# A five-stage network on one core: two weight matrices are converted to float pairs in pieces of 512 columns in place of 256

## The chip, the cores and the metric

The kernel runs on one core of a Trainium2 chip. The metric is the device time of one execution in microseconds (us); the time before is 730.76 us, the median of three runs (730.09 to 730.91). The engines are TensorE (PE in the profile: matrix products; PEld: its weight loads), VectorE (DVE), ScalarE (ACT), GpSimd (POOL) and SyncE (SP), which here does nothing but issue transfers between HBM and the on-chip memory.

## The reference

Three blocks follow one another on 8 sequences of 576 tokens with 512 features. Attention has no softmax: per head `kv = k^T v`, `o = q kv`, and `o` is scaled by the reciprocal root of its mean square. A gated block multiplies `x @ w_val` by the sigmoid of a causal convolution of 5 taps and applies `w_out`. A spatial gating block applies `w_in`, gelu, normalises one half, mixes it over the tokens by `w_sg`, multiplies the other half by it, applies `w_out2` and adds its input:

```
kv = einsum('bhsd,bhse->bhde', k, v);  out = einsum('bhsd,bhde->bhse', q, kv)
x  = out / sqrt(mean(out*out) + 1e-6) * g_norm
x  = (sigmoid(conv5(x)) * (x @ w_val)) @ w_out
h  = gelu(x @ w_in);  u, v = h[:512], h[512:]
v  = w_sg @ normalised(v) + b_sg
return x + (u * v) @ w_out2
```

`w_in` is 512 x 1024 and `w_out2` 512 x 512. They, like `w_val` and `w_out`, come as 64-bit floats.

## The kernel before

TensorE multiplies numbers of a reduced width, so each operand is held as a pair (high and low part), and a product takes three passes (`gemm3`, L228). A 64-bit weight is loaded as pairs of 32-bit words into a tile `raw` (two buffers) and turned into such a pair by `split` in eight steps on a work tile `cv` (one buffer): on ScalarE L131, on VectorE L141, L142 and L134, on ScalarE L178 (the high part is written), on VectorE L143 and L138, on GpSimd L186, and on VectorE L188 (the low part is written). One piece is 128 rows by `WC` columns. `split` returns the load of a piece first and its steps second, so `wi[n][0]()` issues a load and `wi[n][1]()` the steps.

The first part of the kernel is a loop over 8 sequences (b = 0 to 7), each in 8 slots (s = 0 to 7). In slots 0 to 3 PE computes a block of 128 features of `x @ w_val` (val), in slots 4 to 7 one of the product with `w_out` (y). Between these stands the attention of the next sequences: products with k and v (kv, L280), `o` for one tile of 128 tokens (L296), its square on ScalarE (L302), the sum over heads on VectorE (L305), mean and power on GpSimd (L306, then L307), the scaling back on VectorE (L310, which writes a tile T), and the transposes on PE (xT, L325). ScalarE and VectorE take the transposed tile over (L329, L330, L334). When the fifth tile of a sequence is there, ScalarE makes the first tap of its convolution (L353) and VectorE the other four: 16 instructions of line L359 that follow one another, the burst spoken of below. VectorE further does L387 (val times gate) and L391 (low parts; half of these on GpSimd). After b = 3 and b = 7 comes a tail, in which the last 64 tokens of four sequences are handled together (256 columns wide).

Pieces of `w_in` and `w_out2` are converted in the slots that a table gives for each b; their loads are issued two pieces ahead, into the two buffers of `raw`, which the second part uses too (`load_piece`, L452, reads y_main into them). Nothing of `w_in` or `w_out2` is needed before the second part. That begins with products of w_in (hv, L478), at 302.03 us in the profile, and loops over the 8 sequences with hu, sg (L587) and out. All of it is recorded in a program order, and a scheduler then puts the instructions of each engine into an order of its own; each engine works its list in that order, and waits are semaphores.

Of the kernel before, what the change touches and what calls it, by code (L numbers as in the profile page):

```python
# [29 lines left out]
HALO = KC - 1  # L30
CG = math.sqrt(2.0 / math.pi)
AG = 0.044715
WC = 256

LINE = 128
ROOM = {"st": 128, "bst": 32, "bmv": 32, "gcol": 32, "gln": 32, "mhalf": 96, "cw": 64, "T": S, "X32": 19 * 128}
# [6 lines left out]
class Slots:  # L43
# [5 lines left out]
    def later(self, slots, fn, rank=1):  # L49

        self.waiting.append((self.now + slots, rank, fn))

    def tick(self):
        due = [w for w in self.waiting if w[0] <= self.now]
        self.waiting = [w for w in self.waiting if w[0] > self.now]
        for _, _, fn in sorted(due, key=lambda w: w[1]):
            fn()
        self.now += 1
# [7 lines left out]
def body(ctx, tc, qT, k, v, gcol, w_val, conv_w, w_out, w_in, g_ln, w_sgT, b_sg, w_out2, out, out_r):  # L66
# [8 lines left out]
    def sb(tag, shape, dtype=F32, bufs=1, o=0):  # L75
        count[0] += 1
        words = math.prod(shape)
        t = pool.tile([P, o + words], dtype, tag=tag, name=f"{tag}_{count[0]}", bufs=bufs,
                      padded_shape=[P, ROOM.get(tag) or -(-(o + words) // LINE) * LINE])[:, o:]
        if len(shape) == 1:  # L80
            return t
        d = [f"d{i}" for i in range(len(shape))]
        return t.rearrange(f"p ({' '.join(d)}) -> p {' '.join(d)}", **dict(zip(d, shape)))
# [61 lines left out]
    def split(src, h, l, raw=None, tmp=None, k=None, last=nc.gpsimd.tensor_tensor):  # L145
# [10 lines left out]
        def load():  # L156
            r = raw
            if r is None:
                r = sb("raw", [WC * 2], I32 if wide else F32, bufs=2)
            if not wide:  # L160
# [53 lines left out]
    def split_weight(w, src, c0, n):  # L214

        return [split(src[kt * P:(kt + 1) * P, c0 + c:c0 + c + WC], w[:, 0, kt, c:c + WC], w[:, 1, kt, c:c + WC])
                for c in range(0, n, WC) for kt in range(NK)]

# [208 lines left out]
    def sg_weight(stage):  # L427
        p2["sgw"] = sb("WV", [NK + 3, S], F32R)
        p2["sgl"] = sb("G", [NK, S], F32R)
        for t in range(NK):  # L430
            def parts(t=t):
                act(p2["sgw"][:, t], stage[:, t], AF.Copy)
                tt(p2["sgl"][:, t], stage[:, t], f32(p2["sgw"][:, t]), op=ALU.subtract)

            parts()

    def w2_pieces():
        p2["kv"] = [sb(i, [5, D], F32R) for i in "KV"]
        p2["w2"] = w2 = [t[:, :NK] for t in p2["kv"]]
        return [split(w_out2[kt * P:(kt + 1) * P, c:c + WC], w2[0][:, kt, c:c + WC], w2[1][:, kt, c:c + WC])  # L440
                for c in range(0, D, WC) for kt in range(NK)]

    def v_alloc():
        xh, xl, vq = (sb(i, [NK, D], F32R) for i in ("X0h", "X0l", "Q"))
        p2["v"] = [(t[:, i], t[:, i + 1]) for t in (xh, xl, vq) for i in (0, 2)] + [[t[:, 4] for t in p2["kv"]]]
# [173 lines left out]
    def latest():  # L619

        found = {}
        for i in reversed(nc.cur_bb.bb.instructions):
            if i.engine in ELEMENTWISE and i.engine not in found:
                found[i.engine] = i
                if len(found) == len(ELEMENTWISE):
                    break
        return list(found.values())

    def behind(marks, fn):

        with ExitStack() as pins:
            for i in marks:
                pins.enter_context(tc.issue_after(i))
            fn()

    def background(pieces, every, first=1, per=1):

        state = {"i": 0}

        def step():  # L640
            for _ in range(per):
                i = state["i"]
                if i >= len(pieces):
                    return
                if i == 0:
                    pieces[0][0]()
                if i + 1 < len(pieces):
                    pieces[i + 1][0]()
                pieces[i][1]()
                state["i"] += 1  # L650
            later(every, step, 3)

        later(first, step, 3)
# [19 lines left out]
    def taps():  # L673
        if conv_w.dtype == F32:
            dma(cw, conv_w)
            return lambda: None
        raw = sb("raw", [WC * 2], I32, bufs=2)[:, :2 * NK * KC]
        dma(raw, conv_w.bitcast(I32))
# [92 lines left out]
    odd = (1, 3, 5, 7)  # L771
    for b in range(B):
        if b:
            moe = Moe(atts[b].xh, atts[b].xl, gate, y_main[b])
        nxt = atts[b + 1] if b + 1 < B else None
        nn = atts[b + 2] if b + 2 < B else None
        group = b % RG == RG - 1
        if b == 2:
            p2["wiv"], p2["wiu"] = (sb(n, [2, NK, D], F32R) for n in ("wiv", "wiu"))
            wi = split_weight(p2["wiv"], w_in, D, D) + split_weight(p2["wiu"], w_in, 0, D)  # L780
            wi[0][0]()
            wi[1][0]()
            wi_n = 0
        for s in range(8):
            if s < 4:
                if b:
                    moe.val(s)
            else:
                moe.out(s - 4)
            if b == 0 and s in (3, 4):  # L790
                later(0, lambda s=s: behind(marks[0], wo_pieces[s - 1][1]), 3)
            if b == 0 and s < 2:
                nxt.o(s)
            if nxt and s < 3:
                nxt.o(s + 2)
            if nn and (s == 3 or s == 4 and not group):
                nn.kv(s - 3)
            if nn and s == 3:
                nn.load_q()
            if b + 3 < B and s == 5 and not group:  # L800
                atts.append(Attention(b + 3))
                atts[-1].load_kv()
            if nn and s in (6, 7) and not group:
                nn.o(s - 6)
            if nxt and s in (5, 7):
                later(0, lambda a=nxt, m=s - 5: a.gates((m, m + 1)), 2)
            if s == 2:
                later(0, atts[b].rest_parts, 2)
            if (b, s) == (B - 3, 7):
                w2 = w2_pieces()  # L810
                wi += w2[:4]
            if s in {2: (1, 4, 7), 3: odd, 4: odd, 5: odd, 6: odd, 7: (0,)}.get(b, ()):
                later(0, lambda w=wi[wi_n][1], m=marks[-3]: behind(m, w), 3)
                if wi_n + 2 < len(wi):
                    later(0, wi[wi_n + 2][0], 4)
                wi_n += 1
            if b == B - 1:
                if s == 0:
                    v_alloc()
                if s == 4:  # L820
                    stage = sb("X32", [NK, S])
                    dma(stage, w_sgT[:4 * P, :].rearrange("(t p) s -> p t s", p=P))
                    toks = Tokens(0)
                    toks.load(0)
                if s > 4:
                    toks.load(s - 4)
                    later(0, lambda t=s - 5: toks.split(t), 1)
            tick()
            marks.append(latest())
        if group:  # L830
            moe = Moe(rest["x"][:, 0], rest["x"][:, 1], rest["g"], y_rest[b // RG])
            for s in range(8):
                if s < 4:
                    moe.val(s)
                else:
                    moe.out(s - 4)
                if nn and s == 1:
                    nn.kv(1)
                if b + 3 < B and s == 2:
                    atts.append(Attention(b + 3))  # L840
                    atts[-1].load_kv()
                if nn and s == 3:
                    nn.o(0)
                    nn.o(1)
                if b == B - 1:
                    if s == 0:
                        toks.split(3)
                    if s < 4:
                        toks.hv(s)
                    if s == 2:  # L850
                        rem = Rests(0)
                        later(1, rem.split, 1)
                    if s == 4:
                        sg_weight(stage)
                        rest_weight()
                        p2["r"] = sb("X32", [2, 2, D], F32R)
                    if s == 5:
                        y_r = Group.load(0)
                    if s == 6:
                        background(w2[4:], 2, 2)  # L860
                if b == B - 1 or s % 2:
                    tick()

# [106 lines left out]
```

## Time and profile before

| | |
|---|---|
| time, median of 3 runs | 730.76 us (730.09 to 730.91) |
| profiled execution | 731.37 us, of which the span of the trace is 729.6 us |
| PE busy | 715.7 us (98%), 4490 matmuls |
| DVE busy | 583.5 us (80%), 1127 instructions |
| ACT, POOL busy | 351.6 us (48%), 152.9 us (21%) |

The span begins with the first instruction and ends with the last; the profiled execution's own time has 1.8 us more around it. A timeline row is: start in us, duration in us, engine, line, operation, tiles written and read, shapes, count; in brackets the idle time of the engine ahead of it and what ended it. PE's matmuls overlap, and their ends are modelled, so the pace of PE is read from one start to the next and not from durations. A DVE row's duration also reaches a little into the next one; what an instruction costs in a queue is the distance from its start to the start of the next.

### The profile page before, as it was taken

The numbers are of one execution on the slowest core, as the hardware profiler recorded it, in microseconds if no ns is written. First come the engines' busy times: TensorE is split into PE (matmuls) and PEld (weight loads), VectorE is DVE, ScalarE is ACT, GpSimd is POOL, SyncE is SP. The second block draws the span as 40 slices with busy tenths as digits, with TensorE's granted clock in tenths as the row PEclk, the third lists the DMA queues.
The fourth block names the chain that finished last, engine by engine and source line by source line (L and its number), as shares of the span: only waits on it lengthen the run. The fifth ranks groups of instructions, "written<-read, shape, count | busy, mean of one in ns | idle before, by whom it ended". The sixth has DMA issues, their size and how long they took to land.

```text
span 729.6 us, 11757 instructions
## 1 busy us (share of the span) xinstructions
PE 715.7 (98%) x4490; PEld 622.8 (85%) x4490; DVE 583.5 (80%) x1127; ACT 351.6 (48%) x667; POOL 152.9 (21%) x173
## 2 busy tenths in 40 slices
PE   8898999999999999999999999999999999999998
PEld 7686888889888888899889889888899888898897
DVE  6699979899989899699976877867866867867762
ACT  4566475566565575465533533424333424334330
POOL 1405337261727271212010000000100000100000
PEclk9999999999999999999999999999999999999999
DMA  9945253625363202533221221122240122111202
GB/s 314 350 138 202 72 195 133 224 80 192 110 227 137 88 15 81 205 100 118 72 72 58 88 86 46 59 87 59 87 159 29 59 87 69 61 60 44 101 1 87
DMA packets 56712, 81.19 MB, mean 111 GB/s; under 512 B 3664, under 2 KB 29264, under 8 KB 55632
## 3 DMA queue, kind: packets, MB, share of 16 engines
q1 hardware_dynamic: 56656, 80.45, 32.2%
q8 instruction: 35, 0.57, 0.3%
q14 instruction: 21, 0.17, 0.1%
HBM read 61.56 MB, written 18.87 MB: 110 GB/s over the span
## 4 chain that ended last, share of the span: by engine, by line
PE 58%; DVE 1%; DMA 0%; ACT 0%; POOL 0%; issue 0%; POOLq 0%; SPq 0%; DVEq 0%
PE sg L587 16%; PE hv L478 13%; PE out L228 13%; PE hu L228 12%; PE hur L228 2%; PE y L228 1%; PE val L228 1%; DMA raw<-y_main 0%; DVE Z L391 0%; DVE T L387 0%; POOL cv L186 0%; DVE V L188 0%; DVE cv L134 0%; DVE cv L141 0%; ACT X1h L455 0%
## 5 line engine op out<-in xcount | busy, mean ns | idle before, releaser
L359 DVE SCALAR_TENSOR_TENSOR G<-X,cw,G 128x576 f32<-128x576 f32 x128 | 99.6, 829 | 5.9 <-ACT G L353 5.9
L228 PE MATMUL y<-Z,WOh 128*128 128x512 f32 (+1 forms) x320 | 99.2, 383 | 0.0
L490 POOL TENSOR_TENSOR bmv<-bmv,mhalf 128x1 f32<-128x1 f32 x36 | 21.5, 597 | 342.6 <-DVE bmv L489 342.6
L478 PE MATMUL hv<-wiv,X1h 128*128 128x512 f32 x256 | 83.1, 390 | 0.1
L228 PE MATMUL out<-Z,K 128*128 128x512 f32 x256 | 83.0, 389 | 0.0
L228 PE MATMUL hu<-X1h,wiu 128*128 128x512 f32 x256 | 79.2, 391 | 0.0
L307 POOL TENSOR_TENSOR st<-st,mhalf 128x8 f32<-128x8 f32 x40 | 70.1, 1759 | 8.1 <-DVE st L306 5.8
L228 PEld LDWEIGHTS y<-Z,WOh 128*128 128x128 f32 x320 | 58.7, 191 | 9.8
L467 ACT ACTIVATE T<-T 128x512 f32<-128x512 f32 x68 | 43.0, 633 | 45.5 <-DVE T L464 45.3
L228 PE MATMUL y<-Z,WOl 128*128 128x512 f32 (+1 forms) x160 | 59.1, 373 | 0.0
L228 PEld LDWEIGHTS out<-Z,K 128*128 128x128 f32 x256 | 48.0, 188 | 10.0
L478 PEld LDWEIGHTS hv<-wiv,X1h 128*128 128x128 f32 x256 | 47.7, 188 | 10.0 <-ACT X1h L455 0.5
L588 DVE SCALAR_TENSOR_TENSOR T<-sg,gln,WOl 128x288 f32<-128x288 f32 x64 | 32.8, 517 | 26.2 <-PE sg L587 26.2
L228 PEld LDWEIGHTS hu<-X1h,wiu 128*128 128x128 f32 x256 | 46.6, 188 | 8.3
L228 PE MATMUL hu<-X1l,wiu 128*128 128x512 f32 x128 | 50.0, 390 | 0.0
L478 PE MATMUL hv<-wiv,X1l 128*128 128x512 f32 x128 | 49.9, 390 | 0.0
L228 PE MATMUL out<-Z,V 128*128 128x512 f32 x128 | 49.8, 389 | 0.0
L599 ACT ACTIVATE Z<-T 128x512 fp32r<-128x512 f32 x32 | 20.2, 632 | 56.6 <-DVE T L598 56.6
L296 PEld LDWEIGHTS o<-kvbd,Q 128*128 128x128 f32 x320 | 40.3, 191 | 3.6 <-issue 1.4
L296 PE MATMUL o<-kvbd,Q 128*128 128x128 f32 x320 | 40.7, 275 | 1.2 <-DMA Q<-in_qT_dram 1.2
L228 PE MATMUL val<-X0h,WV 128*128 128x512 f32 x128 | 40.8, 400 | 0.0
L228 PE MATMUL val<-X1h,WV 128*128 128x512 f32 x128 | 40.6, 398 | 0.0
(174 smaller groups left out, 1707.2 us busy)
## 6 DMA issues: line engine op xcount, KB each, us to landing
Q<-in_qT_dram SPq DMA_DIRECT2D x8, 1152.0 KB, 5.9
y_main<-Y SPq DMA_DIRECT2D x8, 1024.0 KB, 3.8
raw<-y_main SPq DMA_DIRECT2D x32, 256.0 KB, 3.1
Y<-y_main SPq DMA_DIRECT2D x32, 256.0 KB, 3.9
out_dram<-Y SPq DMA_DIRECT2D x32, 256.0 KB, 2.3
K<-in_k_dram SPq DMA_DIRECT2D x7, 1024.0 KB, 5.5
V<-in_v_dram SPq DMA_DIRECT2D x7, 1024.0 KB, 8.9
raw<-in_w_in_dram SPq DMA_DIRECT2D x16, 256.0 KB, 4.6
```

What stands on the lines that cost most here:

```text
L228: nc.tensor.matmul(ps, lhsT=a[:, kt, msl], rhs=x[:, kt], start=(i == 0), stop=(i == 3 * NK - 1))
L296: nc.tensor.matmul(po[:, j * P:(j + 1) * P], lhsT=self.q[:, j, o:o + P], rhs=bd[:, j, :], start=True, stop=True)
L307: nc.gpsimd.tensor_tensor(st[:, 2], st[:, 1], mhalf, op=ALU.pow)
L359: stt(gate[:, m], x32[:, m, j:j + S], cw3[:, m, j:j + 1], gate[:, m], op0=ALU.mult, op1=ALU.add)
L467: act(w, w, AF.Tanh, scale=CG * AG)
L478: nc.tensor.matmul(ps, lhsT=a[:, kt], rhs=p2["wiv"][:, w, kt], start=(i == 0), stop=(i == 3 * NK - 1))
L490: nc.gpsimd.tensor_tensor(mv[:, 3:4], mv[:, 2:3], mhalf[:, 0:1], op=ALU.pow)
L587: nc.tensor.matmul(ps, lhsT=a[:, msl], rhs=w, start=(n == 0), stop=(n == len(mm) - 1))
L588: later(0, lambda: stt(vs[:, sl], ps, gln_s[:, m:m + 1], p2["bsg"][:, sl], op0=ALU.mult, op1=ALU.add))
L599: act(g[:, 0], x, AF.Copy)
```

## The change

The piece width `WC` becomes 512, so that `w_in` is converted in 8 pieces in place of 16 and `w_out2` in 4 in place of 8. The slot table names 11 slots in place of 20, the first three pieces of `w_out2` (in place of four) are put behind those of `w_in`, the loads of two of them are issued at b = 5, slot 7, and one piece in place of four is left for the end of the loop.

```
-WC = 256
+WC = 512
 ...
             if (b, s) == (B - 3, 7):
                 w2 = w2_pieces()
-                wi += w2[:4]
-            if s in {2: (1, 4, 7), 3: odd, 4: odd, 5: odd, 6: odd, 7: (0,)}.get(b, ()):
+                wi += w2[:3]
+                w2[0][0]()
+                w2[1][0]()
+            if s in {2: (3, 7), 3: (1, 5), 4: (1, 5), 5: (1, 5), 6: (1, 5), 7: (0,)}.get(b, ()):
                 later(0, lambda w=wi[wi_n][1], m=marks[-3]: behind(m, w), 3)
 ...
-                        background(w2[4:], 2, 2)
+                        background(w2[3:], 2, 2)
```

In the order of instructions this shows at two places that the prediction speaks of. The first is VectorE's list in b = 3, from behind the first eight instructions of the burst to the scaling (L310) of the first tile that is transposed in that b. Before:

```order
L305 TENSOR_REDUCE st_1431<-T_1432 128x8
L141 TENSOR_SCALAR cv_1557<-raw_1372 128x256
L142 TENSOR_SCALAR cv_1557<-cv_1557 128x256
L359 SCALAR_TENSOR_TENSOR G_86<-X_12_85,cw_81,G_86 128x576 x3
L305 TENSOR_REDUCE st_1458<-T_1459 128x8
L359 SCALAR_TENSOR_TENSOR G_86<-X_12_85,cw_81,G_86 128x576
L134 SCALAR_TENSOR_TENSOR cv_1557<-cv_1557 128x256
L359 SCALAR_TENSOR_TENSOR G_86<-X_12_85,cw_81,G_86 128x576 x2
L310 TENSOR_TENSOR T_1432<-o_1426,st_1431 128x512
```

The same stretch in the changed kernel, where the numbers of the tiles are others (the tile scaled is T_1420):

```order
L142 TENSOR_SCALAR cv_1464<-cv_1464 128x512
L359 SCALAR_TENSOR_TENSOR G_86<-X_12_85,cw_81,G_86 128x576 x2
L305 TENSOR_REDUCE st_1419<-T_1420 128x8
L359 SCALAR_TENSOR_TENSOR G_86<-X_12_85,cw_81,G_86 128x576 x2
L134 SCALAR_TENSOR_TENSOR cv_1464<-cv_1464 128x512
L359 SCALAR_TENSOR_TENSOR G_86<-X_12_85,cw_81,G_86 128x576
L305 TENSOR_REDUCE st_1446<-T_1447 128x8
L359 SCALAR_TENSOR_TENSOR G_86<-X_12_85,cw_81,G_86 128x576
L387 TENSOR_TENSOR T_1490<-val_1477,G_86 128x512
L359 SCALAR_TENSOR_TENSOR G_86<-X_12_85,cw_81,G_86 128x576
L310 TENSOR_TENSOR T_1420<-o_1414,st_1419 128x512
```

Two narrow steps and a third (L141, L142, L134) have given way to two wide ones (L142, L134), and one more L359 and one L387 stand ahead of the L310. On PE the list between the previous transposes and these holds 20 matmuls of y ahead of the o, where it held 12.

The second place is the tail after b = 3, again VectorE's list, around the L310 of the two tiles that are transposed there one behind the other. Before (tiles T_1891 and T_1898):

```order
L305 TENSOR_REDUCE st_1897<-T_1898 128x8
L359 SCALAR_TENSOR_TENSOR G_86<-X_12_85,cw_81,G_86 128x576
L138 SCALAR_TENSOR_TENSOR cv_1777<-raw_1668,cv_1777 128x256
L391 TENSOR_TENSOR Z_1789<-T_1884,Z_1789 128x256
L387 TENSOR_TENSOR T_1987<-val_1974,G_86 128x512
L188 TENSOR_TENSOR wiv_1140<-cv_1777 128x256
L310 TENSOR_TENSOR T_1891<-o_1885,st_1890 128x512
L305 TENSOR_REDUCE st_1993<-T_1994 128x8
L141 TENSOR_SCALAR cv_2046<-raw_1734 128x256
L142 TENSOR_SCALAR cv_2046<-cv_2046 128x256
L310 TENSOR_TENSOR T_1898<-o_1892,st_1897 128x512
```

And now (tiles T_1855 and T_1862):

```order
L305 TENSOR_REDUCE st_1861<-T_1862 128x8
L359 SCALAR_TENSOR_TENSOR G_86<-X_12_85,cw_81,G_86 128x576
L391 TENSOR_TENSOR Z_1753<-T_1848,Z_1753 128x256
L143 TENSOR_SCALAR cv_2010<-cv_2010 128x512
L387 TENSOR_TENSOR T_1951<-val_1938,G_86 128x512
L310 TENSOR_TENSOR T_1855<-o_1849,st_1854 128x512
L138 SCALAR_TENSOR_TENSOR cv_2010<-raw_1555,cv_2010 128x512
L305 TENSOR_REDUCE st_1957<-T_1958 128x8
L188 TENSOR_TENSOR wiu_1141<-cv_2010 128x512
L310 TENSOR_TENSOR T_1862<-o_1856,st_1861 128x512
```

Wide L138 and L188 now stand between the two L310, where narrow L141 and L142 stood. On GpSimd the wide L186 of the same piece has come in between the two steps L306 and L307 of the second tile:

```order
L306 TENSOR_SCALAR st_1861<-st_1861 128x8
L186 TENSOR_TENSOR cv_2010<-cv_2010,wiu_1141 128x512
L307 TENSOR_TENSOR st_1861<-st_1861,mhalf_73 128x8
L306 TENSOR_SCALAR st_1957<-st_1957 128x8
L307 TENSOR_TENSOR st_1957<-st_1957,mhalf_73 128x8
```

Before, no step of a conversion stood between the L306 and L307 of either tile there.

## Rows read from the trace of the kernel before

**Rows 1.** Busy time, 115 to 302 us: PE, PEld, DVE, ACT, POOL, PEclk, DMA, GB/s

```profile
115.00:302.00 187.00, 185.34 (x1257) 156.02 (x1255) 173.05 (x315) 115.51 (x223) 85.12 (x83) 1.00 0.37 130
```

**Rows 2.** Waits of PE, 115 to 302 us: total, times, longest

```profile
PE xT L325 <- DVE T L310: 1.6, 4, 0.6
```

**Rows 3.** Timeline of PE, around two of these four waits

```profile
111.31 1.05 PE L296 MATMUL o<-kvbd,Q 128*128 128x128 f32 x8
112.11 0.71 PE L228 MATMUL val<-X0h,WV 128*128 128x512 f32 x2
116.16 0.63 PE L325 MATMUL xT<-ident,T 128*128 128x128 f32 x4 [0.17 <-DVE T L310]
...
149.28 0.63 PE L325 MATMUL xT<-ident,T 128*128 128x128 f32 x4 [0.59 <-DVE T L310]
```

**Rows 4.** Timeline of PE, the last matmul ahead of the second part

```profile
301.51 0.39 PE L228 MATMUL y<-Z,WOh 128*128 128x512 f32 x1
```

**Rows 5.** Chain of waits: start, duration, what

```profile
298.09 3.23 DMA raw<-y_main
...
302.03 0.50 PE hv L478
...
303.93 2.74 PE hv L478 x12
...
726.01 0.02 issue
```

**Rows 6.** Timeline of PE, transposes of the fifth tile, b = 1 and b = 2

```profile
100.83 0.60 PE L325 MATMUL xT<-ident,T 128*128 128x128 f32 x4
...
133.56 0.60 PE L325 MATMUL xT<-ident,T 128*128 128x128 f32 x4
```

**Rows 7.** Timeline of DVE, starts of two bursts and steps inside the second

```profile
102.84 4.47 DVE L359 SCALAR_TENSOR_TENSOR G<-X,cw,G 128x576 f32<-128x576 f32 x6 [3.42 <-ACT G L353]
...
135.99 4.46 DVE L359 SCALAR_TENSOR_TENSOR G<-X,cw,G 128x576 f32<-128x576 f32 x6
...
142.75 0.29 DVE L141 TENSOR_SCALAR cv<-raw 128x256 int32<-128x256 int32 x1
...
143.15 2.28 DVE L359 SCALAR_TENSOR_TENSOR G<-X,cw,G 128x576 f32<-128x576 f32 x3
...
146.66 0.42 DVE L134 SCALAR_TENSOR_TENSOR cv<-cv 128x256 int32<-128x256 int32 x1
146.99 1.55 DVE L359 SCALAR_TENSOR_TENSOR G<-X,cw,G 128x576 f32<-128x576 f32 x2
```

**Rows 8.** Groups by shape: busy us, mean ns of one; idle before, releaser

```profile
L134 DVE SCALAR_TENSOR_TENSOR wiv<-wiv 128x512 int32<-128x512 int32 x6 | 4.0, 686 | 0.1
...
L141 DVE TENSOR_SCALAR wiv<-wiu 128x512 int32<-128x512 int32 x4 | 1.7, 424 | 5.4 <-DMA wiu<-in_w_val_dram 5.4
...
L186 POOL TENSOR_TENSOR cv<-cv,K 128x256 f32<-128x256 f32 x8 | 6.5, 811 | 32.7 <-DVE cv L143 23.3 <-ACT K L178 9.4
```

**Rows 9.** Timeline of POOL, DVE and PE in the tail after b = 3

```profile
187.02 1.64 POOL L307 TENSOR_TENSOR st<-st,mhalf 128x8 f32<-128x8 f32 x1
...
189.08 0.68 DVE L310 TENSOR_TENSOR T<-o,st 128x512 f32<-128x512 f32 x1
...
189.33 1.20 PE L325 MATMUL xT<-ident,T 128*128 128x128 f32 x8
```

**Rows 10.** Timeline of PE, kv in one block of 40 and a piece of 8

```profile
200.49 1.39 PE L280 MATMUL kv<-V,K 128*64 128x64 f32 x40
...
204.45 0.45 PE L280 MATMUL kv<-V,K 128*64 128x64 f32 x8
```

**Rows 11.** DMA issues: count, KB each, us to landing

```profile
raw<-in_w_in_dram SPq DMA_DIRECT2D x16, 256.0 KB, 4.6
```

**Rows 12.** Timeline of POOL and DVE at one place in b = 3

```profile
150.48 1.30 POOL L391 TENSOR_TENSOR Z<-T,Z 128x512 fp32r<-128x512 f32 x1 [1.18 <-ACT Z L388]
...
150.96 0.97 DVE L143 TENSOR_SCALAR cv<-cv 128x256 int32<-128x256 int32 x1
```

## The prediction

> **What bounds the kernel now.** I read the busy times by stretch first. From 115 to 302 us, the stretch in which the pieces are converted (before it the lists of all engines but SP's are the same in both kernels), PE is busy for 185.3 of 187 us and VectorE for 173.1 [rows 1]. So PE sets the time and VectorE is close behind it. Then the waits of PE there: one kind, the transposes xT waiting for the scaling L310 on VectorE, 4 times, 1.6 us in all, 0.6 at the longest [rows 2]. The single rows show that this is too little: a bracket counts from the modelled end of the o block (1.05 us after its start), while an o block with no wait behind it gives way after 112.11 - 111.31 = 0.80 us [rows 3]. So each wait costs its bracket and 0.25 more. The four brackets, two of each size shown [rows 3], are 0.17 in b = 2, 0.59 in b = 3, 0.21 in b = 5 and 0.59 in b = 6: 0.42, 0.84, 0.46 and 0.84 us, 2.56 in all. Two smaller ones have no bracket. The eight transposes at 189.33, for two tiles, took 1.20 us [rows 9]; twice the 0.60 of four [rows 6] less 0.25 is 0.95, so the second tile waited about 0.2. The first matmul of the second part starts at 302.03 [rows 5], 0.52 after the y before it [rows 4], and a matmul of 512 columns takes 2.74 / 12 = 0.228 [rows 5]: 0.29 us lost, waiting in the end for a load of y_main into `raw`, issued at 298.09 [rows 5]. From 302.03 to 726.01 the chain of waits is PE alone [rows 5]. So the conversion costs time only where it makes PE wait, and all it can give back is 2.56 + 0.2 + 0.29 = 3.05 us.
>
> **What a piece costs.** On VectorE a narrow L134 takes 146.99 - 146.66 = 0.33 us of the queue, and L141 and L142 together 143.15 - 142.75 = 0.40 [rows 7], so 0.20 each; L143 is taken like them, and L138 and L188 like L134. The wide forms exist in the first stage: L134 686 ns, L141 424 [rows 8], less the same overlap of 0.09 (0.42 against 0.33) 0.60 and 0.33. Two narrow pieces cost 2 x (3 x 0.33 + 3 x 0.20) = 3.2 us, one wide one 3 x 0.60 + 3 x 0.33 = 2.8: VectorE saves 0.4 us twelve times, about 5 us, spread over a stretch that is not bound by it. What counts is what stands ahead of each L310. An L359 costs (4.46 - 0.09) / 6 = 0.73 [rows 7]; L305, L310 and L387 are like a wide L134, 0.60.
>
> **The waits one by one.** A burst can start once ScalarE has made the first tap: 102.84 - 100.83 = 2.01 us after the last transposes where VectorE was idle for it, but 135.99 - 133.56 = 2.43 where a conversion stood in front [rows 6, 7].
> - b = 2: no conversion is left ahead of the first L310 (L141, L142, L134: -0.73). The wait of 0.42 goes.
> - b = 3: the order puts one L359, one L387, a wide L142 and L134 where L141, L142, L134 were: +0.73 + 0.60 + 0.93 - 0.73 = +1.53. The burst starts 0.42 earlier, since hardly a step now stands before it, and PE has 20 matmuls of y in place of 12 between the transposes, 8 x 0.228 = 1.82 us that it now does here. 0.84 + 1.53 - 0.42 - 1.82 = 0.13: -0.71.
> - b = 5: one L359 fewer ahead of the L310 (-0.73), three steps wide (+0.53): -0.20.
> - b = 6: three steps wide (+0.53), 14 matmuls of y in place of 12 (-0.46), start 0.42 earlier: -0.35.
> - The tail after b = 3: from the start of its burst to the second L310 VectorE now does nine wide steps (four of the 0.33 kind, five of the 0.60 kind: 4 x 0.33 + 5 x 0.60 = 4.32) where it did seven narrow ones (4 x 0.20 + 3 x 0.33 = 1.79): +2.53. The start is taken 0.42 earlier. PE gets two more y (0.46), four more transposes of that row (0.2), and ten more matmuls of kv at 1.39 / 40 = 0.035 (0.35) [rows 10]: about 1.0. The second tile's wait grows from 0.2 to 0.2 + 2.53 - 0.42 - 1.0 = 1.3: +1.1. GpSimd agrees: its L307 for that tile stands behind the wide L186, which can begin only after L143. A wide GpSimd product of two tiles takes 1.30 [rows 12], L307 1.64 [rows 9], 2.94 after L143, and VectorE's five steps of 0.60 from L143 to the end of this L310 make 3.0. Behind the waiting transposes stand PE's val matmuls of b = 4, so PE stops.
> - Start of the second part: y_main's first load now reuses a `raw` buffer free since b = 6, not one that a conversion holds until 298: -0.29. Late next would be the second load, which waits for the piece converted in b = 7; by the order two val blocks and the y blocks of b = 7 stand on PE ahead of its reader and cover it.
> - kv: a piece of 8 between y blocks takes 0.45, against 8 x 0.035 = 0.28 inside a block of 40 [rows 10]. The order has 14 such blocks in place of 16: -0.34, bounds 0 and -0.7.
>
> Sum: -0.42 - 0.71 - 0.20 - 0.35 + 1.1 - 0.29 - 0.34 = -1.2 us.
>
> Priced at nothing: ScalarE and GpSimd, which save busy time and are idle for over a third of the stretch [rows 1]. SP's loads move twice the bytes of 256 KB half as often [rows 11]; in the first stage two of them lie in front of k, v, q and w_out, whose readers come several us after they land; without that cover the price would be the time of another 512 KB, under 2 x 4.6 us. The four pieces that ran beside the first sequence of the second part become one; PE did not wait there. What no row shows is a wide L186 with its neighbours: taken at 1.3 us, bounds 0.81 (the narrow one [rows 8]) and 1.62 (two of these).
>
> At one place a row speaks against the wide pieces. In b = 3 a narrow L143 took 0.97 us [rows 12], where a narrow L141 took 0.29 [rows 7], and it ended at 151.93, just after the GpSimd product that ran from 150.48 for 1.30 us [rows 12]. The Trainium skill, "SBUF — State Buffer", section "Who interferes with whom", says that VectorE in a two-port mode or with two inputs in SBUF and a GpSimd instruction that reads SBUF exclude each other, whichever began first, for its whole length. The trace agrees, with 0.68 us of blocking. By the rule one wide L186 can hold up VectorE by 1.3 us where a narrow one could by 0.8; with 0.5 more in the tail the sum would be -0.7.
>
> **The rivals.** (1) All six waits go and nothing new comes: -3.05 - 0.3 (kv) = -3.4 us, 727.4. For it: VectorE has 5 us less to do and half as many chances to be caught by GpSimd. Against it: the order puts the same kind of step ahead of L310 in b = 3, 5 and 6, and wider ones. (2) Slower: the wide L186 ahead of L307 in the tail decides. If the burst there does not start earlier (+0.4), if L307 and L186 take longer beside VectorE (1.62 for 1.3), and if L138 or an L359 is then blocked by GpSimd for as long as L143 was (0.68, for two of them 1.4), the tail's wait becomes 1.3 + 0.4 + 0.3 + 1.4 = 3.4, and the waits of b = 5 and 6 stay (0.55 given up): -1.2 + 2.1 + 0.55 = +1.5, about 732.3. It decides the sign once that wait is over 2.5 us. For it: GpSimd's list. Against: VectorE and GpSimd each only just become the later one there. (3) The waits only move: PE has the same matmuls, each wait that goes comes back at another transpose because the scaler still stands behind a burst of 16; 730.8. For it: 1.6 us of brackets in 187 is already near nothing. Against: the waits of b = 2 and of 302.03 have lost their cause.
>
> **How the numbers follow.** The sum is made on the profiled execution, 731.37 us; that stands 0.6 above the median of 730.76. 731.37 - 1.2 = 730.2 there, 729.6 as a median. The measurement can tell 0.2%, 1.5 us, from no change; the forecast lies inside that. My chances: the forecast with its bounds (728.6 to 730.2) 0.50, of which 0.20 lies under 729.3; rival 1 0.20; rival 2 0.18, of which 0.03 is within 0.2%; rival 3 0.12. So faster 0.40, same 0.45, slower 0.15. The range 727.8 to 732.0 leaves out the ends of rivals 1 and 2.
>
> **What would show it.** In the changed profile: no bracket of xT in b = 2; at most 0.2 in b = 3; brackets of 0.1 and 0.3 in b = 5 and 6; a wait of about 1.3 us at the second transposes in the tail after b = 3, behind an L310 that follows L188; hv following y without a gap; 12 wide L186 of about 1.3 us; PE's waits in this stretch summing to about 2 us in place of 3. The prediction is wrong if PE waits at other places, or if the second part, where I expect nothing, is not as long as before from its first hv to the end.

## The result and the profile after

The changed kernel takes 733.99 us (median of 7 runs, 733.55 to 736.65) where the kernel before takes 730.76 beside it: 1.0054 times as long, interval 1.0040 to 1.0068. That is slower by 0.54%, outside the range I gave. The profiled execution took 733.94 us.

PE's waits between 115 and 302 us come first, since all my terms stand there; busy time of the same stretch under them.

```profile
PE xT L325 <- DVE T L310: 4.4, 4, 2.3
PE val L228 <- DVE T L387: 0.4, 1, 0.4
PE xT L325 <- ACT X L330: 0.3, 1, 0.3
```

```profile
115.00:302.00 187.00, 181.87 (x1243) 153.36 (x1243) 171.97 (x266) 112.86 (x204) 91.45 (x75) 1.00 0.38 133
```

Before, the brackets summed to 1.6 us [rows 2]; now it is 5.1, and PE is busy for 3.5 us less of the stretch than before [rows 1]. The changed kernel has fewer VectorE instructions there (266 for 315), yet VectorE's busy time fell by only 1.1 us, not by the 5 that I had worked out. That 5 was for all twelve pieces; in the loop eleven wide pieces stand for twenty narrow ones, so by my own prices it is 20 x 1.6 - 11 x 2.8 = 1.2 us. GpSimd's busy time, which I had expected to fall, rose by 6.3.

The places, in the timeline of PE after the change (start, duration, operation; in brackets the idle time before it):

```profile
110.96 1.05 PE L296 MATMUL o<-kvbd,Q 128*128 128x128 f32 x8
...
114.59 1.05 PE L296 MATMUL o<-kvbd,Q 128*128 128x128 f32 x8
115.48 0.60 PE L325 MATMUL xT<-ident,T 128*128 128x128 f32 x4
...
146.61 1.05 PE L296 MATMUL o<-kvbd,Q 128*128 128x128 f32 x8
147.53 0.63 PE L325 MATMUL xT<-ident,T 128*128 128x128 f32 x4
...
150.76 1.05 PE L296 MATMUL o<-kvbd,Q 128*128 128x128 f32 x8
152.10 0.63 PE L325 MATMUL xT<-ident,T 128*128 128x128 f32 x4 [0.29 <-ACT X L330]
...
180.61 0.28 PE L228 MATMUL y<-Z,WOl 128*128 128x256 f32 x1
181.33 0.74 PE L228 MATMUL val<-X0h,WV 128*128 128x512 f32 x2 [0.45 <-DVE T L387]
...
188.39 0.60 PE L325 MATMUL xT<-ident,T 128*128 128x128 f32 x4
191.29 0.63 PE L325 MATMUL xT<-ident,T 128*128 128x128 f32 x4 [2.30 <-DVE T L310]
...
225.94 1.05 PE L296 MATMUL o<-kvbd,Q 128*128 128x128 f32 x8
227.00 0.63 PE L325 MATMUL xT<-ident,T 128*128 128x128 f32 x4
...
259.93 0.63 PE L325 MATMUL xT<-ident,T 128*128 128x128 f32 x4 [0.28 <-DVE T L310]
...
267.06 0.39 PE L228 MATMUL val<-X0l,WV 128*128 128x512 f32 x1
267.90 0.63 PE L325 MATMUL xT<-ident,T 128*128 128x128 f32 x4 [0.45 <-DVE T L310]
...
270.25 0.49 PE L228 MATMUL y<-Z,WOh 128*128 128x512 f32 x1
272.09 0.63 PE L325 MATMUL xT<-ident,T 128*128 128x128 f32 x4 [1.34 <-DVE T L310]
...
296.96 0.39 PE L478 MATMUL hv<-wiv,X1h 128*128 128x512 f32 x1
```

A wait is again read from start to start, in us: an o block gives way after 0.80 [rows 3], a matmul of 256 columns after 0.12, one of 512 after 0.23. (With transposes behind it that need not wait, an o block takes some 0.9, so the last 0.1 of such a figure is no wait.)

| place | predicted | measured |
|---|---|---|
| b = 2 | -0.42 | 0.42 to 115.48 - 114.59 - 0.80 = 0.09: -0.33 |
| b = 3, first tile | -0.71 | 0.84 to 147.53 - 146.61 - 0.80 = 0.12: -0.72 |
| b = 3, second tile | 0 | 0.08 to 152.10 - 150.76 - 0.80 = 0.54: +0.46 |
| the values after the tail's y | 0 | 181.33 - 180.61 - 0.12: +0.60 |
| tail after b = 3 | +1.1 | 0.2 to 2.30 + 0.25: +2.35 |
| b = 5 | -0.20 | 0.46 to 227.00 - 225.94 - 0.80 = 0.26: -0.20 |
| b = 6, first tile | -0.35 | 0.84 to 0.53: -0.31 |
| b = 6, later tiles | 0 | 267.90 - 267.06 - 0.23 = 0.61 and 272.09 - 270.25 - 0.23 = 1.61: +2.22 |
| start of the second part | -0.29 | hv stands among y blocks without a gap: -0.29 |
| kv | -0.34 | not read singly |

The rows sum to +3.8 without kv, +3.4 with the forecast for it. The whole path agrees to 0.1: the first block of out in the last group, at the end of the chain of waits, starts here.

```profile
712.49 16.52 PE out L228 x96
```

In the chain of the kernel before it is this one.

```profile
709.49 16.52 PE out L228 x96
```

From the o block of b = 2 (111.31 before [rows 3], 110.96 now) to it there are 598.18 us before and 601.53 after, +3.35; up to that block the profiled execution was 0.35 ahead. The second part itself is as long as before: from 404.83 us on every block of that chain stands 3.00 us later.

The tail on VectorE and GpSimd, after the change:

```profile
169.14 1.74 POOL L186 TENSOR_TENSOR cv<-cv,wiv 128x512 f32<-128x512 f32 x1 [5.27 <-DVE G L359]
169.65 2.57 DVE L359 SCALAR_TENSOR_TENSOR G<-X,cw,G 128x576 f32<-128x576 f32 x2
...
185.21 0.80 DVE L359 SCALAR_TENSOR_TENSOR G<-X,cw,G 128x576 f32<-128x576 f32 x1
...
187.08 1.29 POOL L186 TENSOR_TENSOR cv<-cv,wiu 128x512 f32<-128x512 f32 x1
...
187.80 1.12 DVE L138 SCALAR_TENSOR_TENSOR cv<-raw,cv 128x512 f32<-128x512 uint32 x1
188.33 2.09 POOL L307 TENSOR_TENSOR st<-st,mhalf 128x8 f32<-128x8 f32 x1
...
190.45 0.69 DVE L310 TENSOR_TENSOR T<-o,st 128x512 f32<-128x512 f32 x1 [0.33 <-POOL st L307]
```

Three things are to be seen. VectorE starts the last step of the gates' burst at 185.21; in the kernel before it did at this time:

```profile
185.16 0.80 DVE L359 SCALAR_TENSOR_TENSOR G<-X,cw,G 128x576 f32<-128x576 f32 x1
```

So VectorE had won nothing by then, though its burst had started 2.3 us earlier (166.52 for 168.79), while PE was 0.94 us early (its transposes at 188.39 were at 189.33 before [rows 9]). The L310 came 1.37 later than before (190.45 against 189.08 [rows 9]); 0.94 and 1.37 are 2.3 of the 2.35 us. And the wide L186 is followed by its neighbours: L138 beside it took 1.12 us, not 0.68, and ended 188.92 - 188.37 = 0.55 after it, the L307 behind it 2.09, and the L310 had to wait for that.

### The profile page after: what moved, and what is told of

Read it like the earlier page. It is cut to its first block, busy times and chain, and to the rows that moved or that the text cites. A ratio compares the mean times of both kernels' runs of the same rounds, so it can differ in the third digit from the quotient of the medians.

```text
span 732.1 us, 11595 instructions
## 1 busy us (share of the span) xinstructions
PE 715.2 (98%) x4490; PEld 622.8 (85%) x4490; DVE 577.4 (79%) x1055; ACT 347.1 (47%) x643; POOL 156.4 (21%) x161
## 4 chain that ended last, share of the span: by engine, by line
PE 78%; DVE 13%; issue 2%; POOL 2%; ACT 1%; DVEq 0%; POOLq 0%
PE sg L587 16%; PE out L228 13%; PE hv L478 13%; PE hu L228 12%; PE y L228 9%; PE val L228 8%; DVE G L359 6%; PE o L296 2%; PE xT L325 2%; PE kv L280 2%; PE hur L228 2%; DVE st L305 1%; DVE T L387 1%; DVE T L310 1%; POOL st L307 1%
## 5 line engine op out<-in xcount | busy, mean ns | idle before, releaser
L359 DVE SCALAR_TENSOR_TENSOR G<-X,cw,G 128x576 f32<-128x576 f32 x128 | 101.3, 840 | 8.3 <-ACT G L353 8.3
L307 POOL TENSOR_TENSOR st<-st,mhalf 128x8 f32<-128x8 f32 x40 | 72.2, 1812 | 6.8 <-DVE st L306 4.4
```

The source lines that it names most:

```text
L307: nc.gpsimd.tensor_tensor(st[:, 2], st[:, 1], mhalf, op=ALU.pow)
L359: stt(gate[:, m], x32[:, m, j:j + S], cw3[:, m, j:j + 1], gate[:, m], op0=ALU.mult, op1=ALU.add)
```

## The experiments

Theory P, formed from this profile: the wide GpSimd product L186 makes the new waits, by standing ahead of the powers L307 and by holding VectorE up. Rivals: Q, the wide VectorE steps ahead of an L310 make them; S, the new places in the table do; C, the waits only move. Each ratio is to runs of the kernel before on the same chip; these stood at 730.14 to 730.42, where the expectations reckon from 730.76, so the ratios are the better measure.

**The product left out** (e1 at 512 columns, e2 at 256). L186 and its operation are not issued.

```
- split(..., w[:, 1, kt, c:c + WC])
+ split(..., w[:, 1, kt, c:c + WC], last=lambda *a, **k: None)
```

> The changed kernel (512 columns) without the GpSimd product L186 of the twelve pieces of w_in and w_out2 and of the rest of w_out2: the low part is then the sum of the bits and the low word without the subtraction of the high part (that subtraction is left out). Theory P: the wide L186 makes the new waits, since it stands ahead of the powers L307 on GpSimd and holds up the VectorE step beside it (L138 at 187.80 took 1.12 us for 0.67, L138 at 265.97 1.18). Then the waits of xT at 189, 267 and 270 us (2.55, 0.62, 1.61) mostly go, no L138 takes over 0.8 us, and the time falls from 734.0 to about 730. Rival Q: the wide VectorE steps that stand together ahead of an L310 make them, whatever GpSimd does: only the held-up time of the two L138 goes (about 0.5 us each), and the time stays at 733 or more. Rival S: the pieces' new places in the table make them: also 733 or more.

> The kernel before (256 columns) with the same product L186 left out. Both P and Q: one L138 there is held up by L186 (0.55 us at 203.35) and two L359 by 0.2, and its waits of 0.84 at b = 3 and b = 6 hang on VectorE's queue; so 730 to 731, at most 0.8 below 730.8. If it falls by as much as e1 does (3 us or more), the product costs the same at either width and P is wrong.

At 512 it took 731.49 us, 1.0016 (1.0007 to 1.0024); at 256, 730.67, 1.0009 (0.9999 to 1.0018). Leaving the product out saves nothing that shows at 256 and about 2.8 us at 512 (1.0054 - 1.0016 of 730), less than P's four and more than Q and S allow. The waits of PE at 512:

```profile
PE xT L325 <- ACT Z L388: 1.2, 1, 1.2
PE y L228 <- ACT Z L388: 1.0, 1, 1.0
PE xT L325 <- DVE T L310: 0.6, 2, 0.4
```

The wait of 2.55 in the tail became 0.2 and those of the later tiles of b = 6 went from 2.2 to 0.7 together, as P says, but two others of over 1 us appeared at b = 3 and b = 7. The one at b = 3 stands ahead of the tail and makes PE come later there, so part of what the tail won is only moved. Without any product the wide pieces are still not faster than the narrow ones. The product goes with most of the loss, and does not explain why there is no gain.

**One matrix alone at 512** (e3, e4).

```
  e3: w_in  512 at {2: (3, 7), 3 to 5: (1, 5)},   w_out2 256 at {6: odd}
  e4: w_in  256 at {2 to 5: odd},   w_out2 512 at {6: (1, 5), 7: (0,)}
```

> w_in in pieces of 512 columns at the places of the changed kernel, w_out2 in pieces of 256 at the places of the kernel before in b = 6. All theories that put the waits at 267 and 270 us on the w_out2 pieces: these 2.2 us go and the first wait of b = 6 returns to 0.84 (+0.3), about 732.1; the waits at 181 and 189 us (0.6 and 2.55) stay. Rival C (carry): the waits in b = 6 come from lateness carried over from before: they stay, 734.

> w_in in pieces of 256 columns (at 1, 3, 5, 7 of b = 2 to 5), w_out2 in pieces of 512 at the places of the changed kernel. If the parts add up: the waits at 181 and 189 us are gone, those at 267 and 270 stay: 730.8 + 2.2 - 0.3 - 0.3 (hv) = 732.4. Rival C: 730.8 or less, no wait at 267 and 270.

w_in alone: 733.14, 1.0043 (1.0028 to 1.0057); w_out2 alone: 730.78, 1.0006 (0.9997 to 1.0016). The first kept the waits at 180 and 188 us (0.62 and 2.58) and lost those behind 262, as expected. It is 1 us above my figure: in the profiled execution PE ran at half its clock for a time behind the longer wait (last section), in two other runs the mean clock was low too, and the first wait in b = 6 was 1.3. The second missed by 1.6 us: it has no wait at 267 and 270. Its order shows why it could not have one: the piece that stands between the transposes of b = 6 there is still a narrow one of w_in (L138 is L139 in this kernel):

```profile
265.38 0.41 DVE L139 SCALAR_TENSOR_TENSOR cv<-raw,cv 128x256 f32<-128x256 uint32 x1
```

So this run doesn't test what I meant it to; it shows that wide w_out2 pieces a little later cost next to nothing, which speaks for place and does not prove it.

**Narrow steps at the wide places** (e5): loads and table of the changed kernel, each piece computed in two halves (edit shortened).

```
- st["steps"] = wide_parts(raw, cv)
+ st["halves"] = [wide_parts(raw[c:c + 256], cv[c:c + 256]) for c in (0, 256)]
```

> The changed kernel's loads and places (512 columns), but each piece's steps on all engines in two halves of 256 columns, one after the other. Rival S (the places make the waits): as the changed kernel, 733.5 to 734.5. Rival Q (VectorE's work ahead of an L310): two halves cost VectorE 3.2 us for 2.8, so as slow or slower, 734 to 735. Theory P (one long GpSimd product that VectorE and the powers wait for): a product blocks for 0.8 in place of 1.3 us and the waits at 189, 267 and 270 us shrink by about a third to a half: 732 to 733.

736.17, 1.0083 (1.0068 to 1.0098): the slowest of all, above all three figures. Its waits (L325 and L310 are L337 and L322 here):

```profile
PE xT L337 <- DVE T L322: 6.2, 6, 2.1
```

The tail's wait shrank to 1.1, as P said, but b = 3 had 1.8, b = 5 1.2 and b = 6 up to 2.3. Width as such is not the fault: with the same places and two narrow pieces in each it is worse. Q's reason, that VectorE then has 3.2 us for 2.8 in one place, fits, but GpSimd too has more to do there (two products of 0.8 for one of 1.3), so the run does not part the two. Some of the total is the clock: behind the wait of 2.3 the profiled execution has it at 0.60 from 272 to 276 us.

**The product on VectorE** (e6).

```
- split(..., w[:, 1, kt, c:c + WC])
+ split(..., w[:, 1, kt, c:c + WC], last=tt)
```

> The changed kernel with the product L186 of the pieces on VectorE in place of GpSimd (12 steps of 0.60 us more on VectorE, none on GpSimd). P: no L138 is held up (0.67 us each, where six of twelve took 1.1 to 1.7), L307 is at once behind L306; what VectorE gains from that (about 4 us) it spends on the products (7.2 us), so 731.5 to 733.5, with the tail's wait at 189 us at most 2.3. Q: VectorE is the late one everywhere and gets 0.6 more in each piece: 735 or more.

731.82, 1.0025 (1.0015 to 1.0034), in P's range: though VectorE got 7.2 us more to do, the kernel became about 2 us faster than the changed one. The tail has no wait, though again with a new one of over 1 us at b = 3 ahead of it, so PE's lateness has a part in that. b = 6 has kept its own:

```profile
268.22 0.63 PE L325 MATMUL xT<-ident,T 128*128 128x128 f32 x4 [1.55 <-DVE T L310]
...
271.15 0.63 PE L325 MATMUL xT<-ident,T 128*128 128x128 f32 x4 [0.24 <-DVE T L310]
```

From start to start these are 2.1 us, for 2.2 in the changed kernel. So at b = 6 it does not help to take the product from GpSimd, where leaving it out altogether (e1) did: on either engine it stands ahead of the same L310. All of the order may move in this run, so the next two change less.

**The tail alone**, the product of the one piece there moved to VectorE; and the GpSimd product alone cut in two (edits in short).

```
e9:   last=tt for the first piece of w_in's second half, GpSimd for the others
e10:  last(a[:, e], a[:, e], h[:, e])  for e in the two halves of 256
```

> The changed kernel with one instruction moved from GpSimd to VectorE: the product L186 of the one piece in the tail after b = 3. The order differs there alone: between the two L310 VectorE has L138, L186, L305 for L138, L305, L188, three wide steps either way, and on GpSimd the L307 of the second tile stands right behind its L306. P: L138 is not held up (-0.5) and the L310 does not wait for L307 (-0.35): the wait of 2.55 us at 189 becomes about 1.7, total 733.1. Q (only VectorE's own steps count): the same number of steps, so 2.3 to 2.6 and 734.0.

> The changed kernel with the GpSimd product L186 alone cut into two of 256 columns, in the same order; VectorE's and ScalarE's steps stay 512 wide. If the tail's wait hangs on the time the product takes in GpSimd's queue ahead of L307: two halves take 2 x 0.74 = 1.5 for 1.3 us, the wait grows by 0.2 to 0.3, total 734.0 to 734.5. If it hangs on VectorE being held up by one long product: L138 comes in between the halves, its excess falls from 0.5 to about 0.2, total 733 to 733.5.

e9: 732.35, 1.0034 (1.0022 to 1.0047). Its tail:

```profile
186.35 1.64 POOL L307 TENSOR_TENSOR st<-st,mhalf 128x8 f32<-128x8 f32 x1
187.06 0.68 DVE L138 SCALAR_TENSOR_TENSOR cv<-raw,cv 128x512 f32<-128x512 uint32 x1
187.66 0.68 DVE L186 TENSOR_TENSOR cv<-cv,wiu 128x512 f32<-128x512 f32 x1
188.86 0.68 DVE L310 TENSOR_TENSOR T<-o,st 128x512 f32<-128x512 f32 x1
189.68 0.63 PE L325 MATMUL xT<-ident,T 128*128 128x128 f32 x4 [1.48 <-DVE T L310]
```

The wait is 1.73, as P had it (1.7), and PE's other waits are those of the changed kernel: with as many VectorE steps between the two L310, 0.8 us of the tail's loss belongs to GpSimd. (The two ratios' intervals overlap; the claim rests on the wait.) e10: 733.62, 1.0048 (1.0035 to 1.0061). Its tail (L186, L307, L310 and L325 are L188, L309, L312 and L327):

```profile
185.79 1.98 POOL L188 TENSOR_TENSOR cv<-cv,wiu 128x256 f32<-128x256 f32 x2
186.51 0.67 DVE L138 SCALAR_TENSOR_TENSOR cv<-raw,cv 128x512 f32<-128x512 uint32 x1
187.74 1.63 POOL L309 TENSOR_TENSOR st<-st,mhalf 128x8 f32<-128x8 f32 x1
190.24 0.63 PE L327 MATMUL xT<-ident,T 128*128 128x128 f32 x4 [2.59 <-DVE T L312]
```

L138 is not held up at all, and the wait still grew from 2.55 to 2.84, with the halves at 1.98 us together where I had 1.5; its L310 (L312) waited 0.44 for that L307. So in the tail it is GpSimd's queue ahead of L307 that counts, and not that VectorE is held up there. The total lies between the two forecasts: in b = 6, where the order changed against my expectation, 1.2 us of waits stood in place of 2.2.

**Other places** for the wide pieces, all steps as in the changed kernel.

```
  changed: {2: (3, 7), 3: (1, 5), 4: (1, 5), 5: (1, 5), 6: (1, 5), 7: (0,)}
  e7:      {2: (3, 7), 3: (1, 5), 4: (3, 6), 5: (1, 5), 6: (1, 5), 7: (0,)}
  e8:      {2: (3, 7), 3: (1, 5), 4: (3, 6), 5: (1, 5), 6: (3, 6), 7: (0,)}
  e11:     {2: (3, 7), 3: (1, 5), 4: (3, 6), 5: (1, 5), 6: (3, 7), 7: (1,)}
  e12:     {2: (3, 7), 3: (1, 4), 4: (3, 6), 5: (1, 5), 6: (3, 7), 7: (0,)}
```

> The changed kernel with the two places in b = 4 set from 1 and 5 to 3 and 6, so that no piece is converted in the tail after b = 3; the order from b = 5 on is nearly that of the changed kernel. P and Q: the wait of 2.55 us at 189 falls to 0.2, those of b = 6 stay: 731.6. Rival C (the waits only move): PE's time comes back at the next waits, in b = 4 to 6: 733.5 to 734.

> As e7, and the two places in b = 6 set from 1 and 5 to 3 and 6, so that the w_out2 pieces are converted behind the transposes at 267 and 270 us. P and Q: those two waits (2.2 us) go as well, and the gains forecast at b = 2, 5, 6 and at the start of the second part stay: 729.5. Rival C: 731.5 or more.

> As e8, with the last two of the three w_out2 pieces at 7 of b = 6 and 1 of b = 7 in place of 6 and 0: the wait of 1.1 us that e8 had at 268 (y for the low part L391 on GpSimd, which stands there behind the product of a piece) stays, since the first piece has not moved; the later ones come into a stretch without waits: 729.0 to 729.5. Rival C: 730 or more, with new waits from 275 on.

> As e11 (b = 7 at 0), with the second place of b = 3 at 4 in place of 5, so that the piece there is through before the burst of the tail and fewer of its steps stand ahead of the values of the rest: the waits of e8 at 187 (0.8) and of the changed kernel at 181 (0.6, gone in e8) fall to 0.2: 728.8. Rival C: as e8, 729.5, since VectorE has the same work by 187.

e7: 730.50, 1.0011 (1.0001 to 1.0022), 1.1 below my figure: with the piece out of the tail the wait at 181 goes too, the one at 189 falls to 0.7 (0.2 forecast), and b = 6 has about 1.9 in place of 2.2. C is out: the time did not come back. e8: 729.46, 0.9989 (0.9978 to 0.9999), as expected (729.5). The waits at 267 and 270 are gone, and PE now waits once for GpSimd, as this timeline of e8 shows:

```profile
266.56 1.30 POOL L186 TENSOR_TENSOR cv<-cv,K 128x512 f32<-128x512 f32 x1
267.81 1.72 POOL L391 TENSOR_TENSOR Z<-T,Z 128x512 fp32r<-128x512 f32 x1
269.58 0.73 PE L228 MATMUL y<-Z,WOh 128*128 128x512 f32 x2 [0.97 <-POOL Z L391]
```

So the same wide pieces, with two in b = 4 and two in b = 6 moved by one or two slots, no longer lose anything: this is what shows the places as the cause. e11: 729.65, 0.9996 (0.9987 to 1.0005); e12: 729.55, 0.9995 (0.9986 to 1.0004). Both missed their forecasts, and neither is better than e8; the wait at 187 stayed at 0.7 in both, so e12's forecast of 0.2 was wrong and its rival right. e8 is the only version here whose interval lies below 1, by 0.1% and only just; places that beat the kernel before clearly were not found.

## Why the prediction was wrong

**Right**: the terms for b = 2, the first tile of b = 3, b = 5, the first tile of b = 6 and the start of the second part came as worked out or nearly so (0.33, 0.72, 0.20, 0.31 and 0.29 gained for 0.42, 0.71, 0.20, 0.35 and 0.29); nothing was lost in the second part; the worst wait came where I put it, behind an L310 that follows L188 and an L307 that follows the wide L186.

**The step that failed first is "The tail after b = 3"**, +1.1 predicted and, with the wait at 181 that belongs to it, +2.95 measured. By its own terms: I gave VectorE 2.53 us more from the start of its burst to the second L310. In the traces the burst starts at 168.79 before and 166.52 after, so those stretches (to the L310 at 189.08 and at 190.45) are 20.3 and 23.9 us, +3.6. Of the extra 1.1, the trace shows 1.0 beside GpSimd's instructions: hold-ups inside the burst took 1.7 us (1.0 of it in the two L359 that stand beside the L186 of 169.14, 2.57 for 1.54) where they took 1.5 before, L138 took 1.12 for 0.68, and L310 waited 0.33 for L307. I had this mechanism and its price (0.5 under the sum, 1.4 in rival 2) and left it out of the forecast, with one narrow row to go by. e9 shows 0.8 us of the wait as GpSimd's, e10 that it is the queue ahead of L307. And I let PE's own extra work cover 1.0 us. PE did come 1.0 later, but 0.6 of that is the wait at 181, which is itself a loss, and which I had put at nothing; e7, with no piece in the tail, does not have it.

**The second is that "b = 6" ends at its first tile.** I followed the order ahead of the first L310 only. Behind it the same piece's L143, L138 and L188 stand between the L310 of the later tiles, in a place where VectorE has val, sums and low parts to do as well; +2.2 us, for which I had no term. Two of these steps took 0.5 us more than their 0.68, beside an L186 and an L391 on GpSimd:

```profile
265.97 1.18 DVE L138 SCALAR_TENSOR_TENSOR cv<-raw,cv 128x512 f32<-128x512 uint32 x1
...
269.59 1.15 DVE L188 TENSOR_TENSOR V<-cv 128x512 fp32r<-128x512 f32 x1
```

e1, without the product, keeps 0.7 of the 2.2, and e6, with the product on VectorE, 2.1, so how it divides between the two engines is not settled. e8 shows that it is the place: with the first of these pieces two slots later and the second one slot later the waits are gone.

**The third is that "b = 3" ends at its first tile too.** That one came as worked out (0.12 for 0.13); the second, for which I had no term, waits 0.54 where it waited 0.08. Its bracket names ScalarE's L330, which ended at 152.00, 0.05 us behind VectorE's L310. Both came late behind these two (L330 stands in ScalarE's list behind an L362 that waited for that L359):

```profile
147.30 1.46 DVE L143 TENSOR_SCALAR cv<-cv 128x512 int32<-128x512 int32 x1
...
149.28 1.48 DVE L359 SCALAR_TENSOR_TENSOR G<-X,cw,G 128x576 f32<-128x576 f32 x1
```

Undisturbed they take 0.41 and 0.81. On GpSimd an L391 ran beside the first (147.20 to 148.48) and the piece's L186 beside the second (148.84 to 150.14). The row of the narrow L143 [rows 12] spoke for this, at this place. No run isolates it.

Two readings behind the sum were wrong as well. VectorE does not get 5 us freer in this stretch but 1.2 by my own prices, as said above. And GpSimd, priced at nothing because it would save busy time, was busy for 6.3 us more: where its instructions and VectorE's met, one of the two took longer. The eleven pieces' L138 average 1.02 us where an undisturbed one takes 0.68.

```profile
L138 DVE SCALAR_TENSOR_TENSOR cv<-raw,cv 128x512 f32<-128x512 uint32 x11 | 11.2, 1020 | 0.0
L186 POOL TENSOR_TENSOR cv<-cv,wiv 128x512 f32<-128x512 f32 x4 | 6.5, 1632 | 8.5 <-DVE G L359 5.3 <-DVE cv L143 3.2
```

(Groups by shape of the changed kernel; count, busy, mean ns.) L138 and L186 can both begin once L143 is done, so they often meet: in six of the eleven pieces L138 was held up (1.12 to 1.73 us), in three others L186 was (1.74 to 2.21). I had taken 1.3 us for a wide L186 and called 1.62 its upper bound; the w_in pieces of the first half average 1.63.

**The rivals.** Rival 2 had the sign, the place and the mechanism of the largest wait, and a chance of 0.18. Of its conditions, L186 in the tail took 1.29 and not 1.62, and the waits of b = 5 and the first of b = 6 did not stay; it was short by the waits at 181 and in the later tiles of b = 6. Rival 3 was right in one point: PE's lead up to the tail, 0.94 us, came back there as a wait, because VectorE had not become earlier. Rival 1 is out. Not settled: how much of the tail's remaining 1.7 us is VectorE's wide steps and how much PE's lead, how the 2.2 us of b = 6 divide, and the cause of the waits that e1 and e6 got at b = 3.

The Trainium skill, "SBUF — State Buffer", section "Who interferes with whom", says that a VectorE instruction with two inputs in SBUF and a GpSimd instruction that reads SBUF contend for a shared pair of ports, and that the pair is an exclusive lock. The traces agree: in the six pieces in which L138 was held up it ended 0.54 to 0.56 us after L186 (1.12 for 0.68 in the tail), and in the three in which L186 took longer a VectorE instruction with two inputs had begun just before it.

## What to carry to other kernels

When pieces of a background job are doubled, their number halves but each stands at its place with all its steps: follow every wait of the bounding engine that the piece spans, not only the first one behind it, and on every in-order queue it passes, the one with the short steps on the way to that engine (here L307) above all. A total such as "5 us less for VectorE" says little: first count which pieces still lie in the stretch, then read what they buy at the place where the two engines meet. Two steps that one event releases on VectorE and GpSimd can run at the same time; here they got in each other's way in nine of eleven pieces, so their interference belongs in the sum. And before giving up a larger piece, try it at other places: here one or two slots made up the whole loss.

## What the runs showed of the hardware

After some of its long waits TensorE ran on at its lower clock. In the run with w_in alone PE waited 2.58 us at 188; the granted clock, the last figure but two of this row, was then

```profile
191.00:195.00 4.00, 4.00 (x13) 3.22 (x12) 2.94 (x5) 1.27 (x2) 1.94 (x2) 0.59 0.41 157
```

while the profiled execution of the changed kernel, which had waited 2.55 at the same place, has this one:

```profile
191.00:195.00 4.00, 3.71 (x21) 3.24 (x22) 3.02 (x7) 1.83 (x3) 2.68 (x2) 1.00 0.60 209
```

In the first, matmuls of 512 columns followed each other every 0.43 us for 0.23, eight of them, 1.6 us: 1.2 GHz for 2.4. The halved product of e10 (2.84 us of wait) shows it too, at 0.57 in the same stretch, and e5 behind a wait of 2.3 us, at 0.60 from 272 to 276. So such a wait can cost some 1.6 us more than itself, and it need not: one execution of each kernel was traced, and 2.3 us was followed by the lower clock in one where 2.55 was not in another. A low clock in a trace also need not belong to the change: the profiled execution of e7 took 733.81 us for a median of 730.50 and had the clock at 0.58 from 64 to 72 us, ahead of every piece.
